# First stage of a fused attention, FFN and experts kernel: one hand-written order of single-engine parts for all engines

## The chip, the cores and the metric

The kernel runs on one core of a Trainium2 chip. The metric is device time in microseconds (us): the median of several runs of the whole program.

## What is computed

A bidirectional attention between tokens and 32 state slots, a two-layer FFN with g = h - tanh(h), and a gated mixture of eight experts, all in float32:

```python
scores = scale * x @ state.T          # softmax over slots, then a @ state
scores2 = scale * state @ x.T         # softmax over tokens, then a2 @ x
x = concatenate([xread, sread])       # 2304 tokens, 512 wide
h = x @ w_in                          # 512 -> 2048
x = (h - tanh(h)) @ w_out             # 2048 -> 512
out = sum over e of P[:, e] * (relu(x @ w1[e]) @ w2[e])
```

There are B = 4 batches of H = 8 heads, S = 512 tokens, D = 64.

## The kernel before, in words

Products run with float32r operands that are split into a high and a low part, so each is three matmuls (`mm3`, lines 92 to 95: high by high, low by high, high by low). The FFN is cut into NJ = 8 slices j of 256 columns. Slice j = 0 is run together with the attention; that is the first stage, and the one that the change touches.

**Attention of a batch** (class `Attention`, lines 265 to 363). `tokens(p)` turns two heads of x on TensorE (tile xtps) and copies them out (xt). `scores(q)` multiplies them with the state (sc2ps), copies the result (sc) and takes the largest (mx). `over_slots(half)` turns the scores (sc1ps), takes the largest over slots (m) and subtracts it (e). `exps` does the exponentials on ScalarE, the sums and reciprocals on VectorE and the share e times m on GpSimd (L320). `back(q)` turns the other softmax (e2ps, e2t). `weights(q)` turns the shares (atps) and splits them: ath on ScalarE (L89), then atl = atps - ath on VectorE (L90). `read(q)` multiplies the token softmax with x (srps) and writes four narrow pieces of 32x64 into yacc_s, scaled by sm, on ScalarE (L359).

**First products.** `emit_m(j, bp, q)` multiplies w_in with the state of a pair of batches (mps; mh on ScalarE, ml on VectorE). `emit_h(j, b, i)` multiplies ath, atl with mh, ml (hps) and makes the gate t = h - tanh(h) and its split gh, gl. `emit_y(0, b, d)` multiplies gh, gl with w_out (yps) and copies the sum to yacc. `emit_xs` and `emit_hs` do the same for the 128 state rows (xsps, hsps), and `emit_ts` turns their gate (tsps). The first tsps of the program comes at the end of the stage.

**Weight pieces.** The weights of the FFN come as 64-bit words in pieces of 128x256. `prep()` (lines 155 to 206) is one step of a pipeline over pieces: ScalarE makes mag and low (L203, L204), VectorE makes mag, low and bits (L187, L194, L190), GpSimd adds (L198), ScalarE casts the high part (L182), GpSimd subtracts for the low part (L165). Each slice takes 8 pieces; `prep_done` and `tick` call prep ahead of their use.

**What sets the order.** The steps of the stage are written batch by batch (`first_unit`, lines 580 to 617): while a batch's attention is finished the next one is begun. Each step holds work of several engines. The program is put in order by a planner with a timeline of its own, which moves instructions within what their data allow; `anchor` and `behind` keep some prep steps behind the last instruction traced on ScalarE and VectorE. x of batches 0 and 1 is loaded on SP (`load_x`, L224), and the state on ScalarE's DMA queue (L232); the state rows are copied into slb by four VectorE and four ScalarE copies (L241). The first ScalarE copy also brings an ACT_TABLE_LOAD.

After the first stage, slices 1 to 7 of the FFN and then the experts follow; those loops are not touched, except for the bound that `most` sets for prep, which is written in other units.

## Time and profile before

| | us |
|---|---|
| median of 3 runs | 1790.05 (1788.44 to 1791.13) |
| the profiled execution | 1788.31 |
| its span | 1786.5 |
| TensorE busy in the span | 1753.3 (98%) |
| VectorE busy | 1188.8 (67%) |
| ScalarE busy | 803.5 (45%) |
| GpSimd busy | 1191.6 (67%) |

The span is the stretch that the profile sees on the core; the execution's own time is 1.8 us more. PE is TensorE, PEld its weight loads, DVE VectorE, ACT ScalarE, POOL GpSimd, SP the queue that issues most DMAs. The busy shares are over the whole span; the first stage is its first 118.7 us, in which the engines stand otherwise.

### The profile page before, as it was taken

What the parts mean: (1) busy time and instruction counts of PE and PEld (TensorE: products, weight loads), DVE (VectorE), ACT (ScalarE), POOL (GpSimd) and SP (SyncE); (2) the same over time, 40 slices, a digit from 0 to 9 for tenths busy, and PEclk for the clock granted to TensorE, in tenths of its full rate; (3) what the DMA queues carried; (4) which work ended last, traced back from release to release, by engine and by line L of the source; (5) the groups of instructions that cost most, each with busy time, mean ns of one, the idle gap of its engine ahead of it and who ended that gap; (6) DMA issues with size and microseconds to landing.
All of it is one profiled execution on the core that took longest, in us unless ns stands there. A gap on an engine that the chain in (4) does not pass through costs nothing.

```text
span 1786.5 us, 23142 instructions
## 1 busy us (share of the span) xinstructions
PE 1753.3 (98%) x8181; PEld 1444.3 (81%) x8181; DVE 1188.8 (67%) x1762; ACT 803.5 (45%) x1429; POOL 1191.6 (67%) x1041
## 2 busy tenths in 40 slices
PE   7899999999999999999999999999999999999998
PEld 4578888877888888888888888888888888888887
DVE  6688887555876666666666666856666666666665
ACT  7877666545233323333232333344444445444442
POOL 3366555457777767666667776557777777777774
PEclk9999999999999999999999999999999999999999
DMA  5311110007666666555665665555555655645541
GB/s 142 90 59 66 59 48 19 0 30 238 208 204 218 212 206 204 197 196 202 203 199 192 203 212 188 195 200 200 218 184 189 234 181 190 230 175 202 212 183 53
DMA packets 158695, 296.73 MB, mean 166 GB/s; under 512 B 28340, under 2 KB 107764, under 8 KB 154228
## 3 DMA queue, kind: packets, MB, share of 16 engines
q1 hardware_dynamic: 157540, 295.00, 48.3%
q8 instruction: 64, 1.05, 0.2%
q14 instruction: 51, 0.42, 0.1%
q10 hardware_dynamic: 1040, 0.26, 0.1%
HBM read 174.87 MB, written 120.36 MB: 165 GB/s over the span
## 4 chain that ended last, share of the span: by engine, by line
PE 87%; DVE 6%; ACT 3%; POOL 2%; issue 1%; DMA 1%; DVEq 0%; ACTq 0%
PE p1b L978 14%; PE p_P L1129 14%; PE p1a L978 9%; PE p1c L978 9%; PE p L95 7%; PE p L93 7%; PE p L94 7%; PE yps L94 2%; PE yps L93 2%; PE yps L95 2%; PE p1s L1030 2%; PE mP L1129 2%; DVE low L194 1%; PE hps L95 1%; PE hps L93 1%
## 5 line engine op out<-in xcount | busy, mean ns | idle before, releaser
L771 POOL TENSOR_TENSOR w1l<-w1r,w1h 128x768 fp32r<-128x768 f32 (+1 forms) x96 | 170.9, 1807 | 159.9 <-ACT w1h L769 159.9
L1081 DVE SCALAR_TENSOR_TENSOR oacc<-p,pr,oacc 128x512 f32<-128x512 f32 x224 | 166.2, 744 | 111.9 <-PE p L95 111.9
L978 PE MATMUL p1b<-xT,w1h 128*128 128x512 f32 x768 | 237.6, 390 | 0.0
L1138 DVE TENSOR_TENSOR m<-p_P,m 128x512 f32<-128x512 f32 x232 | 159.3, 688 | 86.8 <-PE p_P L1129 86.8
L93 PE MATMUL p<-w2b,hh 128*128 128x512 f32 x512 | 199.9, 390 | 1.8 <-ACT hh L916 1.5
L94 PE MATMUL p<-w2b,hh 128*128 128x512 f32 x512 | 199.4, 389 | 0.0
L95 PE MATMUL p<-w2b,hl 128*128 128x512 f32 x512 | 197.1, 390 | 0.6 <-DVE hl L917 0.6
L986 DVE TENSOR_TENSOR U<-p1b,P 128x512 f32<-128x512 f32 x128 | 88.4, 690 | 150.2 <-PE p1b L978 128.3
L978 PEld LDWEIGHTS p1b<-xT,w1h 128*128 128x128 f32 x768 | 142.4, 188 | 28.0
L978 PE MATMUL p1a<-xB,w1h 128*128 128x512 f32 x512 | 161.1, 395 | 0.0
L411 POOL TENSOR_TENSOR gl<-t,gh 128x512 fp32r<-128x512 f32 x64 | 86.4, 1361 | 101.8 <-ACT gh L410 100.6
L978 PE MATMUL p1b<-xT,w1l 128*128 128x512 f32 x384 | 149.6, 390 | 0.0
L806 ACT CAST w2s<-w2r 128x1024 fp32r<-128x1024 f32 x32 | 33.7, 1052 | 229.6 <-POOL w2r L800 229.6
L935 POOL TENSOR_TENSOR h11l<-U,h11h 128x512 fp32r<-128x512 f32 x32 | 41.4, 1294 | 126.8 <-ACT h11h L934 82.1
L917 DVE SCALAR_TENSOR_TENSOR hl<-U,hh 128x512 fp32r<-128x512 f32 x64 | 101.2, 1581 | 27.9 <-ACT hh L916 27.9
L1136 ACT COPY m<-p_P 128x512 f32<-128x512 f32 x128 | 74.9, 586 | 99.9 <-PE p_P L1129 99.6
L93 PEld LDWEIGHTS p<-w2b,hh 128*128 128x128 f32 x512 | 96.1, 188 | 23.0 <-ACT hh L916 2.6
L95 PEld LDWEIGHTS p<-w2b,hl 128*128 128x128 f32 x512 | 96.1, 188 | 21.1 <-DVE hl L917 1.3
L768 POOL TENSOR_TENSOR w1r<-w1r 128x256 f32<-128x256 f32 x128 | 94.2, 746 | 27.1 <-DMA w1r<-in_moe_w_dram 24.2
L94 PEld LDWEIGHTS p<-w2b,hh 128*128 128x128 f32 x512 | 96.1, 188 | 19.7
L986 DVE TENSOR_TENSOR U<-p1c,U 128x512 f32<-128x512 f32 x128 | 87.7, 685 | 33.6 <-PE p1c L978 33.3
L978 PEld LDWEIGHTS p1a<-xB,w1h 128*128 128x128 f32 x512 | 93.7, 188 | 17.8
(297 smaller groups left out, 4810.2 us busy)
## 6 DMA issues: line engine op xcount, KB each, us to landing
w1h<-w1h SPq DMA_DIRECT2D x64, 896.0 KB, 4.3
w1l<-w1l SPq DMA_DIRECT2D x64, 896.0 KB, 6.1
w<-w2a SPq DMA_DIRECT2D x30, 1024.0 KB, 4.8
w<-w2c SPq DMA_DIRECT2D x30, 768.0 KB, 7.6
w1r<-in_moe_w_dram SPq DMA_DIRECT2D x128, 128.0 KB, 4.4
w2r<-in_moe_w_dram SPq DMA_DIRECT2D x32, 512.0 KB, 4.0
w2a<-w2b SPq DMA_DIRECT2D x60, 256.0 KB, 3.3
w2c<-w2s SPq DMA_DIRECT2D x60, 256.0 KB, 3.9
```

Of the source, the lines that this page charges most:

```text
L93: nc.tensor.matmul(ps, whi, xhi, start=start, stop=False, **k)
L94: nc.tensor.matmul(ps, whi, xlo, start=False, stop=False, **k)
L95: nc.tensor.matmul(ps, wlo, xhi, start=False, stop=stop, **k)
L411: nc.gpsimd.tensor_tensor(out=lo, in0=g, in1=f32(hi), op=ALU.subtract)
L768: nc.gpsimd.tensor_tensor(out=r[:, out], in0=r[:, a], in1=r[:, b], op=op)
L771: nc.gpsimd.tensor_tensor(out=lo[:, c0:c1], in0=r[:, c0:c1], in1=f32(hi[:, c0:c1]), op=ALU.subtract)
L917: nc.vector.scalar_tensor_tensor(out=lo, in0=src, scalar=0.0, in1=f32(hi), op0=ALU.max, op1=ALU.subtract)
L978: nc.tensor.matmul(t[z], w[:, slot, k, :], x[:, m, k, :], start=(first and k == i == 0), stop=(k == 1 and i == 2), skip_group_check=True,)
L986: nc.vector.tensor_tensor(out=t[name], in0=a, in1=b, op=ALU.add)
L1081: nc.vector.scalar_tensor_tensor(out=o, in0=ps, scalar=w, in1=o, op0=ALU.mult, op1=ALU.add)
L1129: nc.tensor.matmul(ps, w[:, a], b, start=(i == 0 and not goes_on), stop=(i == 2 and (last or not kept)), skip_group_check=True,)
L1138: nc.vector.tensor_tensor(out=m, in0=ps, in1=m, op=ALU.add)
```

## The change

All steps of the first stage are cut into parts that each hold work of one engine (`words_of`, `bits_of`, `number_of`, `hi_of`, `lo_of` for a weight piece; `tokens` and `keep_tokens`, `weights`, `weights_hi` and `weights_lo`, and so on for the attention and the products). A table of 440 words, ORDER_OF_FIRST, names them in one order: a word is the part's letter, the batch (or slice and batch) and an index, and at times the engine that does it (A, V or G). `listed` runs a part with each of its instructions pinned behind the last instruction traced so far on its engine, for all five engines, so that the parts of the table keep their order on every engine. Other instructions may still be moved between them by the planner.

The work itself is the same but for these: of the copies out of PSUM, 4 of 16 of xt, 3 of 8 of e2t (1 of 8 before) and 4 of 16 of yacc are done by DVE; 20 of the 32 narrow products into yacc_s move from ACT to DVE; one of the eight state copies moves to DVE; a copy of one column of `ones` at the start brings the ACT table load ahead of the state copies; x of batches 0 and 1 is loaded by head, 8 DMAs each, batch 1 first (before: 8 halves for batch 0, 4 DMAs for batch 1). The pieces 0 to 15 are in the table; prep goes on from piece 16. Batches 1 and 0 are run interleaved, then 2 and 3.

```diff
         live = {}
-        at = [0]
-        rest = [-1] * 4
-        steps_of = [*range(KD), *rest, *range(KD, 2 * KD), *rest, *range(2 * KD, len(pieces))]
+        FIRST_PIECES = 4 * KD
+        at = [FIRST_PIECES]

         def piece(step):
-            return steps_of[step] if 0 <= step < len(steps_of) else -1
+            return step if FIRST_PIECES <= step < len(pieces) else -1

...
+        def words_of(n):
+            v = live[n]
+            nc.scalar.activation(temp(n, "mag", F32, 2), f32(v["raw"][:, :, 1]), AF.Abs, scale=REBASE)
+            nc.scalar.mul(temp(n, "low", U32, 3), v["raw"][:, :, 0], 2.0 ** -29)
...
+        def number_of(n):
+            v = live[n]
+            nc.gpsimd.tensor_tensor(out=v["bits"], in0=v["bits"], in1=v["low"], op=ALU.add)
...
-                )
-                nc.gpsimd.tensor_tensor(out=t, in0=t, in1=v["low"], op=ALU.add)
-            n = piece(step)
-            if n >= 0:
-                fetch(n + AHEAD)
-                v = live[n]
-                nc.scalar.activation(temp(n, "mag", F32, 2), f32(v["raw"][:, :, 1]), AF.Abs, scale=REBASE)
-                nc.scalar.mul(temp(n, "low", U32, 3), v["raw"][:, :, 0], 2.0 ** -29)
+            for part, behind in (((lo_of,), 4), ((hi_of,), 3), ((bits_of, number_of), 1), ((words_of,), 0)):
...
         def prep_done(n):

-            while at[0] < n + 12:
+            while at[0] < n + 4:
                 prep()


...
+        def load_x(b, i):
+
             if b not in x_t:
                 x_t[b] = att.tile([P, NT, H, D], F32, tag="x", bufs=2, name=f"x{b}")
-            for h in range(0, H, heads):
-                for t in range(NT):
-                    nc.sync.dma_start(
-                        x_t[b][:, t, h:h + heads], x[b, h:h + heads].rearrange("h (p t) d -> t p h d", t=NT)[t]
-                    )
-                yield
+            if b > 1:
+                nc.sync.dma_start(x_t[b][:, i], x[b].rearrange("h (p t) d -> t p h d", t=NT)[i])
+            else:
+                nc.sync.dma_start(x_t[b][:, :, i], x[b, i].rearrange("(p t) d -> p t d", t=NT))
...
         for be in range(2):
             for r in range(4):
                 u, w = divmod(r, 2)
                 to = 2 * ((u + be) % 2) + w
-                (nc.scalar.copy if be else nc.vector.tensor_copy)(
+                (nc.scalar.copy if be and r else nc.vector.tensor_copy)(
                     slb[NS * to:NS * (to + 1), :, u::2, w * D:(w + 1) * D], srow[NS * r:NS * (r + 1), be::2]
                 )
-        for n in range(AHEAD + 3):
-            fetch(n)
-        run(load_x(1), 9)
-
...
             def weights(self, q):
-                b = self.b
-                ps = bank(f"atps{b}_{q}")
+                ps = self.ps["w", q] = bank(f"atps{self.b}_{q}")
                 for t in range(NT):
                     g = self.e1[t // 2][0].rearrange("a g s -> a (g s)")
                     o = (t % 2) * 256 + q * P
                     nc.tensor.transpose(ps[:, t * P:(t + 1) * P], g[:, o:o + P], ident)
-                hi = ffn.tile([P, S], F32R, tag="ath", bufs=B * NQ, name=f"ath{b}_{q}")
-                lo = ffn.tile([P, S], F32R, tag="atl", bufs=B * NQ, name=f"atl{b}_{q}")
-                split_ps(ps, hi, lo)
-                at_t[b, q] = hi, lo
+
+            def weights_hi(self, q):
+                hi = ffn.tile([P, S], F32R, tag="ath", bufs=B * NQ, name=f"ath{self.b}_{q}")
+                lo = ffn.tile([P, S], F32R, tag="atl", bufs=B * NQ, name=f"atl{self.b}_{q}")
+                at_t[self.b, q] = hi, lo
+                nc.scalar.copy(hi, self.ps["w", q])
+
+            def weights_lo(self, q):
+                hi, lo = at_t[self.b, q]
+                nc.vector.tensor_tensor(out=lo, in0=self.ps.pop(("w", q)), in1=f32(hi), op=ALU.subtract)

...
+            def keep_read(self, q, by_scalar):
+                b, ps = self.b, self.ps.pop(("r", q))
                 for r in range(4):
                     h = 4 * q + 2 * ((r // 2 + b) % 2) + r % 2
-                    nc.scalar.mul(
-                        sr[NS * b:NS * (b + 1), h * D:(h + 1) * D],
-                        ps[NS * r:NS * (r + 1), r % 2 * D:(r % 2 + 1) * D],
-                        self.sm[NS * r:NS * (r + 1), q:q + 1],
-                    )
-
...
+        def y_first(b, d):
+            ps = laid[0, b, d] = acc_bank(f"yps0_{b}_{d}")
+            for i in range(2):
+                wh, wl = wo_t[i]
+                mm3(ps, wh[:, d * P:(d + 1) * P], wl[:, d * P:(d + 1) * P], *g_t[0, b, i], i == 0, i == 1)
+
+        def y_keep(b, d, copy):
+            copy(yacc[b][:, d, :], laid.pop((0, b, d)))

...
-        def first_unit(b):
...
-        def anchor():
-            for z, e in (("ACT", mybir.EngineType.Activation), ("DVE", mybir.EngineType.DVE)):
-                last[z] = next(i for i in reversed(nc.cur_bb.bb.instructions) if i.engine == e)
-
-        def behind(fn):
-
-            with tc.issue_after(last["ACT"]), tc.issue_after(last["DVE"]):
+        att_t = {}
+        ENGINES = [getattr(mybir.EngineType, z) for z in ("PE", "Activation", "DVE", "Pool", "SP")]
+
+        def listed(fn):
+
+
+            traced = nc.cur_bb.bb.instructions
+            with ExitStack() as pins:
+                for e in ENGINES:
+                    mine = next((i for i in reversed(traced) if i.engine == e), None)
+                    if mine is not None:
+                        pins.enter_context(tc.issue_after(mine))
                 fn()

-        for b in range(-1, B - 2):
-            for n, step in enumerate(first_unit(b)):
-                step()
-                if n == 5 if b < 0 and at[0] < 16 else n % 4 == 3:
-                    anchor()
-                if b < 0 and at[0] < 16 and n > 5:
-                    behind(prep)
-                elif (b >= 0 or n > 5) and n % 4 == 3:
-                    behind(tick)
-        for step in first_unit(B - 2):
-            step()
-        for j in range(NJ):
...
+            PARTS[z] = lambda b, n, fn=fn: fn(10 * b + n)
+        PARTS["Y"] = y_first
+        PARTS["x"] = load_x
+
+        ORDER_OF_FIRST = """
+            x16 x10 x12 x11 x14 x13 x17 x15 F02 T10 U00 t10A F01 U10 u00 v00 x01 T11 v10 u10 T13 x03 t11A V10
+            x02 t13A T12 V00 S10 A02 x00 t12V x05 A01 I02 S11 x06 c10 I01 F03 j02 c11 T01 F12 C02 m10 j01 O10
...
+            q40 Y32 y30A Y33 y32A y33A
+        """
+        for word in ORDER_OF_FIRST.split():
+            listed(lambda: PARTS[word[0] + word[3:]](int(word[1]), int(word[2])))
+        att_ctx.close()
+        emit_ts(0)
+        emit_hs(1)
+        for j in range(1, NJ):
             more = j + 1 < NJ
-            if j:
-                most[0] = 8 * (j + 2) + 2 + 11
+            most[0] = 8 * (j + 2) + 2 + 3
             if not more:
                 mid_ctx.close()
                 x2p = ctx.enter_context(right("x2p", reuse_waits="tile"))
...
@@ -669,24 +778,12 @@
                     [lambda: emit_logits_of_operands(1)], [lambda: emit_logits(2)],
                 ]
             for b in range(B):
-                if j == 0 and b < B - 1:
-                    continue
                 steps = {d: [] for d in range(KD)}
                 if b + 1 < B:
                     steps[0] += [lambda i=i: emit_h(j, b + 1, i) for i in range(2)]
                 elif more:
-                    steps[0 if j else 2] += [lambda i=i: emit_h(j + 1, 0, i) for i in range(2)]
-                if j == 0:
-                    emit_xs()
-                    att_ctx.close()
-                    emit_hs(0)
-                    most[0] = 29
-                    prep_done(16)
-                    for q in range(NQ):
-                        steps[0].append(lambda q=q: emit_m(1, 0, q))
-                        steps[1].append(lambda q=q: emit_m(1, 1, q))
-                    steps[3].append(lambda: emit_ts(0))
-                elif more and b == B - 2:
+                    steps[0] += [lambda i=i: emit_h(j + 1, 0, i) for i in range(2)]
+                if more and b == B - 2:
                     prep_done(8 * (j + 1) + KD)
                     for q in range(NQ):
                         steps[q].append(lambda q=q: emit_m(j + 1, 0, q))
```

Three places show how instructions move. In the rows a name ends in its index and a number of its buffer.

DVE, batch 1's attention weights (atl is the low part of the weights, ath the high part that ACT casts just before; m and e are the softmax over slots, mx the largest score, ml the low part of the first product; mag, low and bits belong to a weight piece). Before:

```order
L318 TENSOR_SCALAR m_1_1_512<-m_1_1_512 128x16
L190 TENSOR_SCALAR bits_595<-mag_537 128x256
L319 RECIPROCAL m_1_0_503<-m_1_0_503 128x16
L319 RECIPROCAL m_1_1_512<-m_1_1_512 128x16
L90 TENSOR_TENSOR atl_0_619<-atps_0_613,ath_0_618 128x512
L90 TENSOR_TENSOR atl_1_635<-atps_1_629,ath_1_634 128x512
L187 TENSOR_SCALAR mag_602<-mag_602 128x256
```

Now:

```order
L306 TENSOR_REDUCE mx_0_203<-sc2ps_1_330 128x1
L161 TENSOR_SCALAR mag_320<-mag_320 128x256
L164 SCALAR_TENSOR_TENSOR low_322<-raw_256,low_322 128x256
L168 TENSOR_SCALAR bits_371<-mag_320 128x256
L322 TENSOR_REDUCE m_0_1_385<-sc1ps_1_359 128x16
L310 TENSOR_SCALAR mx_0_203<-mx_0_203 128x1
L391 TENSOR_TENSOR atl_0_388<-atps_0_375,ath_0_387 128x512
L328 TENSOR_TENSOR e_0_1_411<-sc1ps_1_359,m_0_1_385 128x512
L391 TENSOR_TENSOR atl_1_403<-atps_1_380,ath_1_402 128x512
L450 TENSOR_TENSOR ml_1_392<-mps_1_1_393,mh_1_391 64x512 x2
```

Before, the two atl follow the reciprocals of their own batch; now parts of batch 0 (mx_0, m_0, e_0) and a weight piece stand between them.

PE, the end of the stage (yps is the second product of the FFN, hps the first one of the next slice, tsps the turn of the state rows' gate, hsps the state rows' product of slice 1). Before:

```order
L94 MATMUL yps_3_3_1363<-gl_3_1_1160,woh_441 128x512
L95 MATMUL yps_3_3_1363<-gh_3_1_1159,wol_442 128x512
L93 MATMUL hps_0_0_1320<-ath_1_331,mh_0_1241 128x512
L94 MATMUL hps_0_0_1320<-atl_1_332,mh_0_1241 128x512
L93 MATMUL hps_0_1_1334<-ath_0_322,mh_0_1241 128x512
```

Now:

```order
L95 MATMUL hps_0_0_1245<-ath_1_630,ml_0_1046 128x512
L93 MATMUL yps_1_0_1255<-gh_1_0_692,woh_664 128x512
L94 MATMUL yps_1_0_1255<-gl_1_0_693,woh_664 128x512
L95 MATMUL yps_1_0_1255<-gh_1_0_692,wol_665 128x512
L93 MATMUL yps_1_0_1255<-gh_1_1_593,woh_640 128x512
L94 MATMUL yps_1_0_1255<-gl_1_1_594,woh_640 128x512
L95 MATMUL yps_1_0_1255<-gh_1_1_593,wol_641 128x512
L559 MATMUL tsps_1308<-ident,ts_1091 128x128 x2
```

Before, only batch 3's second product was left at the end of the stage; now products of batch 1 (yps_1) come as late as that, and some of batch 3 come behind tsps.

DVE, behind the last atl of the stage, where no attention is left (t is the gate; the pieces with raw_1383 and up are numbers 16 and up, which belong to slice 2). Before:

```order
L90 TENSOR_TENSOR atl_1_1098<-atps_1_1092,ath_1_1097 128x512
L518 MEMSET wg 128x512
L523 MEMSET wg_both 128x512
L530 TENSOR_TENSOR add<-ident 16x8
L90 TENSOR_TENSOR xs_lo<-xsps,xs_hi 128x512
```

Now, some rows further on:

```order
L164 SCALAR_TENSOR_TENSOR low_1389<-raw_1383,low_1389 128x256
L468 TENSOR_TENSOR t_3_1_1136<-hps_3_1_1103,t_3_1_1136 128x512
L161 TENSOR_SCALAR mag_1387<-mag_1387 128x256
L168 TENSOR_SCALAR bits_1415<-mag_1387 128x256
L450 TENSOR_TENSOR ml_1_1144<-mps_1_0_1145,mh_1_1143 64x512 x2
L516 COPY yacc_80<-yps_2_3_1167 128x512
L161 TENSOR_SCALAR mag_1424<-mag_1424 128x256
```

The planner puts pieces 16 and up, which are not in the table, between the table's parts here, and the xs and wg instructions now stand ahead of the last atl. From the middle of slice 1 on, the instructions stand alike in both programs on every engine.

## Rows read from the trace of the kernel before

**Rows 1.** The page's first part: busy time, share and instructions of each engine.

```profile
PE 1753.3 (98%) x8181; PEld 1444.3 (81%) x8181; DVE 1188.8 (67%) x1762; ACT 803.5 (45%) x1429; POOL 1191.6 (67%) x1041
```

**Rows 2.** Windows: stretch, its length, busy of PE, PEld, DVE, ACT, POOL, clock, DMA.

```profile
0.00:14.60 14.60, 7.39 (x29) 4.57 (x30) 6.20 (x14) 7.14 (x14) 1.56 (x8) 1.00 1.03 228
14.60:102.40 87.80, 72.28 (x433) 51.50 (x431) 61.16 (x143) 71.42 (x173) 38.12 (x44) 0.92 0.34 89
102.40:118.60 16.20, 15.90 (x88) 13.58 (x89) 14.07 (x26) 14.39 (x34) 8.43 (x10) 1.00 0.10 30
118.60:162.00 43.40, 42.97 (x214) 36.25 (x213) 38.07 (x67) 31.38 (x72) 28.01 (x30) 1.00 0.19 63
```

**Rows 3.** The chain that ended last, 98 to 120 us: start, us, what.

```profile
101.11 0.59 ACT ath L89
101.73 0.70 DVE atl L90
...
116.01 0.23 PE yps L95
...
118.73 0.23 PE tsps L452 x2
```

**Rows 4.** Waits, 14.6 to 102.4 us: total, times, longest.

```profile
DVE atl L90 <- ACT ath L89: 16.9, 3, 7.5
...
DVE mx L290 <- ACT sc L288: 5.8, 4, 2.3
...
DVE m L303 <- PE sc1ps L299: 2.8, 1, 2.8
```

**Rows 5.** Timeline of DVE, 48 to 64 us: start, us, instruction, [idle before, releaser].

```profile
52.95 0.36 DVE L319 RECIPROCAL m<-m 128x16 f32<-128x16 f32 x2
60.78 1.29 DVE L90 TENSOR_TENSOR atl<-atps,ath 128x512 fp32r<-128x512 f32 x2 [7.47 <-ACT ath L89]
```

**Rows 6.** DVE's groups, 0 to 118.6 us: count, busy, mean ns, idle before.

```profile
L194 DVE SCALAR_TENSOR_TENSOR low<-raw,low 128x256 uint32<-128x256 uint32 x22 | 11.4, 525 | 0.1
...
L187 DVE TENSOR_SCALAR mag<-mag 128x256 f32<-128x256 f32 x23 | 10.1, 447 | 0.5 <-ACT mag L203 0.4
L190 DVE TENSOR_SCALAR bits<-mag 128x256 uint32<-128x256 uint32 x22 | 9.9, 461 | 0.5 <-POOL wil L165 0.3
...
L291 DVE TENSOR_SCALAR mx<-mx 128x1 f32<-128x1 f32 x8 | 1.2, 151 | 0.2
...
L331 DVE COPY e2t<-e2ps 128x512 f32<-128x512 f32 x1 | 0.7, 676 | 0.0
...
L518 DVE MEMSET wg<- 128x512 f32 x1 | 0.5, 485 | 0.1
```

**Rows 7.** ACT's groups, 0 to 118.6 us.

```profile
L203 ACT ACTIVATE mag<-raw 128x256 f32<-128x256 f32 x24 | 10.3, 439 | 0.1
...
L359 ACT ACTIVATE yacc_s<-srps,sm 32x64 f32<-32x64 f32 x32 | 9.8, 305 | 5.4 <-PE srps L353 3.3 <-issue 1.7
...
L279 ACT COPY xt<-xtps 128x512 f32<-128x512 f32 x16 | 9.2, 596 | 2.2 <-PE xtps L277 2.2
L436 ACT COPY yacc<-yps 128x512 f32<-128x512 f32 x16 | 8.5, 592 | 3.8 <-PE yps L95 3.7
...
...
L241 ACT ACT_TABLE_LOAD x1 | 1.3, 1283 | 5.0 <-DMA yacc<-in_state_dram 5.0
```

**Rows 8.** Timeline of SP's queue, 0 to 30 us.

```profile
0.74 5.03 SPq L224 DMA_DIRECT2D x<-in_x_dram  x8
...
8.26 5.21 SPq L224 DMA_DIRECT2D x<-in_x_dram  x4
```

**Rows 9.** Tile bits, 0 to 118.6 us: duration ns min/median/max, first and last start.

```profile
L190 DVE TENSOR_SCALAR bits<-mag x22: 278/285/1385, 12.9 to 116.8; 128x256 uint32<-128x256 uint32 x22
```

**Rows 10.** Windows of the two stretches at the lower clock.

```profile
25.60:32.40 6.80, 6.24 (x23) 5.41 (x24) 6.61 (x13) 5.02 (x14) 2.06 (x3) 0.50 0.16 49
...
52.90:59.80 6.90, 4.91 (x30) 3.94 (x32) 0.40 (x3) 2.85 (x7) 2.73 (x3) 0.51 0.12 40
```

More of the change, by code (lines that the diff above doesn't have):

```diff
@@ L199, in prep @@
-            n = piece(step)
-            if n >= 0:
-                fetch(n + AHEAD)
-                v = live[n]
-                nc.scalar.activation(temp(n, "mag", F32, 2), f32(v["raw"][:, :, 1]), AF.Abs, scale=REBASE)
-                nc.scalar.mul(temp(n, "low", U32, 3), v["raw"][:, :, 0], 2.0 ** -29)
+            for part, behind in (((lo_of,), 4), ((hi_of,), 3), ((bits_of, number_of), 1), ((words_of,), 0)):
+                n = piece(step - behind)
+                if n >= 0:
+                    if not behind:
+                        fetch(n)
+                        fetch(n + AHEAD)
+                    for fn in part:
+                        fn(n)
@@ L234, in attention_ffn_experts @@
         )
-        for _ in first:
-            pass
+        nc.scalar.copy(ones[:, :1], ones[:, :1])
         for be in range(2):
@@ L305, in over_slots @@
[L305 to L322 removed]
+                self.ps["o", half] = v, m
@@ L571, in turn_logits @@
             )
-        most = [3 * KD + 2 + 12]
+        most = [0]
         def tick():
@@ new lines, in of_batch, with part @@
+        def of_batch(name, *more):
+            def part(b, n):
+                if b not in att_t:
+                    att_t[b] = Attention(b)
+                getattr(att_t[b], name)(n, *more)
+            return part
+        COPY = {"A": nc.scalar.copy, "V": nc.vector.tensor_copy}
+        ON = {"V": nc.vector, "G": nc.gpsimd}
+        PARTS = {z: of_batch(name) for z, name in (
[3 rows of a table added]
+        )}
+        for z, copy in COPY.items():
+            PARTS["t" + z] = of_batch("keep_tokens", copy)
+            PARTS["b" + z] = of_batch("keep_back", copy)
+            PARTS["g" + z] = of_batch("keep_read", z == "A")
+            PARTS["y" + z] = lambda b, d, copy=copy: y_keep(b, d, copy)
```

329 lines of the change are left out of this document (183 added, 146 removed), and 3 rows, old and new, of the table PARTS.

## The prediction

> **What bounds the kernel now.** I read the page first: PE is busy in 98% of the span [rows 1], so the stages behind the first give nothing back and pass a gain on whole; they keep their instructions. Then the windows by stage, which show that the first stage is another matter. I cut it at three points. Until 14.6 us the data arrive and the first scores are made. From there to 102.4 lies the attention: it ends with the last atl, which runs from 101.73 for 0.70 [rows 3]. From 102.4 to 118.6 only products are left, and at 118.73 the first tsps starts [rows 3], which I take as the end of the stage in both programs. In the middle stretch of 87.80 us ACT is busy for 71.42 (81%), PE for 72.28, DVE for 61.16 (70%) [rows 2]: no engine is full. The waits say why. DVE idles 87.80 - 61.16 = 26.6 us, of which 16.9 stand in three waits of atl for ath, 5.8 in four of mx for the score copy, 2.8 in one of m [rows 4], together 25.5. The longest is seen in DVE's timeline: it ends batch 1's reciprocals at 53.3 and does nothing for 7.47 us, until ath is there at 60.78 [rows 5]. Softmax, turn, cast and split follow one another in one batch, and the queue holds nothing else that could run. So the stage is bound by chains that hand over from engine to engine.
>
> **The change, term by term.** I sum against the profiled execution, 1788.31 us; it is 1.74 below the median of 1790.05, which I add again at the end. PE's matmuls are the same in number and kind, so are POOL's instructions; what changes is the place.
>
> *DVE in the attention part.* Counted in the two orders up to the last atl, DVE loses 9 low, 8 mag and 6 bits, since only 12 pieces are done there (before some 20): 9 x 0.525 + 8 x 0.447 + 6 x 0.461 = 11.1 us [rows 6]. It gains 7 wide copies, 7 x 0.676 = 4.7 (e2t's copy, rows 6), and 20 narrow products. DVE's price for these is not in the trace: below lies mx of one column with 0.151 [rows 6], above ACT's price for the same piece, 0.305 [rows 7], so 3.0 to 6.1. I take 0.22, between them, because DVE's wide operations cost about what ACT's do: 4.4. One more state copy, the two fills of wg (0.485 each, rows 6) and xs_lo, which now stand earlier, make 2.0. So 11.1 go and 11.1 come, and DVE keeps its 6.20 + 61.16 = 67.4 us [rows 2].
>
> *ACT and PE there.* ACT loses 15 mag and low at 0.44, 16 narrow products at 0.305, 4 xt copies at 0.596 and 9 yacc copies at 0.592 [rows 7], 19.2 us, and some 4 us of smaller moves: of its 78.6 us [rows 2] about 56 stay. Of the 96 matmuls of the second product, PE does 24 there instead of 72: 48 at 0.23 [rows 3], 11.0 us less. So DVE becomes the busiest engine and sets the length.
>
> *How much DVE still idles.* This term decides. In the new order parts of the other batch and a weight piece stand between reciprocals and atl; the two batches of a pair alternate, so the wait of one is filled by the other. Bounds: 0, if every wait is filled; 26.6, if all stay. The nearest rows are those where DVE has independent work: in 102.4 to 118.6 it idles 2.1 of 16.2 us, in 118.6 to 162 5.3 of 43.4, 12 to 13% [rows 2], and there PE holds it up. I take a quarter of 26.6, 6.6 us, which is a tenth of the new stretch.
>
> *Lead-in.* ACT_TABLE_LOAD stands between the landing of the state and ACT's state copies with 1.28 us [rows 7]; it moves ahead of the landing. The x loads limit what follows: 8 issues took 5.03 us, the 4 larger ones of batch 1 5.21 [rows 8], so 16 small ones cost SP the same, and the first batch arrives no sooner. I count 1.0 of the 1.28: 14.6 becomes 13.6. The weight pieces are issued later now, behind batch 1's x; their first use (mps) is behind both batches' scores, which hides that. If that cover fails, the first mps waits for the issues that are now ahead of its pieces, 0.63 us for each (5.03 / 8).
>
> *End of the attention part:* 13.6 + (67.4 - 6.2) + 6.6 = 81.4, where before 102.4 stood: -21.0.
>
> *The products behind it.* They took 16.2 us, PE busy for 15.90 [rows 2]. The 11.0 us of deferred second products come on top: 27.2. DVE does 14.07 now, and gets some 10 us of pieces 16 and up, which the planner hoisted; less gates and fills it has about 22 in 27.2 and stays covered. If a hoisted piece stands ahead of a gate that PE needs, that cover is gone; I add 0.5. Then tsps starts at 81.4 + 27.2 + 0.5 = 109.1, against 118.7: **-9.6 us**. Slice 1 gets the same pieces as before, so nothing is given back there. 1788.31 - 9.6 = 1778.7 for the profiled execution, with the 1.74 **1780.4 us** for the median.
>
> *The clock.* In two stretches of 6.8 and 6.9 us the granted clock was 0.50 and 0.51 [rows 10], the level of 1.2 GHz; PE was busy 6.24 and 4.91 us in them. At the full clock half of that, 5.6 us, would be saved if it lay on the path. In the new attention part DVE sets the length, so I count 0 and keep 5.6 for a rival. The Trainium skill (TensorE: Matmul & The Clock Gate, What's actually happening) has the low clock as the default that activity releases; by it a denser PE would lose both falls, and the sum would be nearer to that rival.
>
> **Rivals.**
>
> *B, the fill is nearly complete and DVE gets cheaper.* bits took 0.461 us in the mean, but 0.285 in the median and up to 1.385 [rows 9]: some of the piece operations are stretched. In the attention part their number falls to 36, and POOL has a third fewer pieces to do there. If all 36 were stretched as bits is and none of it were left, 36 x 0.176 = 6.3 us would go; with the idle time at 3 instead of 6.6 and the clock kept up the gain is 9.6 + 3.6 + up to 6.3, 13 to 19.5: 1770.5 to 1777, say 1774. Against it: the stage gets shorter and POOL's 48.1 us [rows 2] do not, so both are busy together more of the time.
>
> *C, the busiest engine alone counts.* Before, ACT with 78.6 us made an attention part of 102.4; DVE with 67.4 at the same share makes 87.8, and with 27.7 behind it 115.5: -3.2, 1786.9, within what can be told from no change. The Trainium skill (Perfetto Trace Analysis, Identifying the Most-Contended Engine) has kernels improve by their most-contended engine, and by that rule this would be the result. For it: balancing moved 11 us on to DVE. Against it: the longest waits stand on an engine that was not the busiest.
>
> *D, slower: the fixed order brings its own waits.* A part that is late holds everything behind it on its engine, and the planner may no longer go around it. The place is DVE behind ACT's casts: narrow products wait for PE's reads, atl for ath, with the other batch's largest scores behind them. If as much idle time is left as before (26.6), the attention part ends at 13.6 + 61.2 + 26.6 = 101.4, and 27.7 behind it makes 129.1: +10.4, 1800. It decides from 16.2 us of idle time on, where the sum is zero.
>
> *E, the hoisted pieces hold up the gates.* Half of their 10 us on PE's path in the last stretch makes 109.1 + 5 = 114.1: -4.6, 1785.4.
>
> That the order is not followed is excluded: the orders of the engines show it.
>
> **How the numbers follow.** My forecast A (idle time from 4 to 10 us) has 0.50, B 0.22, C 0.12, E 0.08, D 0.08. A measurement of this kernel can tell about 0.2%, 3.6 us, from no change, so faster begins below 1786.5. A, B and E lie there: 0.80; C makes 0.12 for the same, D 0.08 for slower. The range of A is 1777 to 1784. The range goes down to 1771, into B but not to its end, and up to 1788, over E and C; D and the ends of B and C are left out, some 0.18.
>
> **What would show it.** Right: the first tsps near 109 us and the last atl near 81; DVE's idle time between 13.6 and there under 10, no wait of atl over 2 us; the stage's gain equal to the gain of the span within 1 us. Wrong: a last atl behind 90 with waits of DVE for ACT in the list (C or D), an early last atl with a tsps that does not follow within 29 us (E), or a later stage that idles longer than before.

## The result, and the profile after

The changed kernel takes **1775.39 us** (median of 6 runs, 1774.96 to 1775.92), the kernel before, on the same chip, 1790.49 (6 runs, 1787.95 to 1791.13): ratio 0.9919, 95% interval 0.9906 to 0.9932, so 15.1 us less. Of the profiled executions, before took 1788.31 with a span of 1786.5 and the changed one 1775.18 with 1773.4: 13.1 us less.

The first part of the page of the changed kernel, beside [rows 1]:

```profile
span 1773.4 us, 23139 instructions
PE 1747.0 (99%) x8181; PEld 1441.1 (81%) x8181; DVE 1201.2 (68%) x1793; ACT 794.3 (45%) x1399; POOL 1193.5 (67%) x1041
```

As many matmuls, but PE is busy for 6.3 us less. PE's busy time counts the matmuls at the low clock with their longer duration, and one of the two falls of [rows 10] is gone (below). Half of the busy time in the falls is what they add: 5.6 us before, 1.7 now, so 3.9 of the 6.3; the rest is not accounted for.

To say where the 13.1 us come from, a mark is needed at which both programs have done the same work. The first turn of the token sums (tsps), which the prediction took, is not such a mark. In the order of PE's matmuls, 24 second products (yps) that stood ahead of it before stand behind it now; at the second turn 7 matmuls still do (1 yps, 6 of the state rows' ysps); at the third the two programs have run the same matmuls. PE's timeline around the three turns, before and after:

```profile
118.57 0.38 PE L452 MATMUL tsps<-ident,ts 128*128 128x128 f32 x2
125.53 0.38 PE L452 MATMUL tsps<-ident,ts 128*128 128x128 f32 x2
166.92 0.38 PE L452 MATMUL tsps<-ident,ts 128*128 128x128 f32 x2
```

```profile
99.16 0.38 PE L559 MATMUL tsps<-ident,ts 128*128 128x128 f32 x2
111.07 0.38 PE L559 MATMUL tsps<-ident,ts 128*128 128x128 f32 x2
154.03 0.38 PE L559 MATMUL tsps<-ident,ts 128*128 128x128 f32 x2
```

Third turn: 166.92 - 154.03 = **12.9 us**, beside 13.1 of the span. So the whole gain lies ahead of it, and the later slices keep it. At the first turn, with 24 x 0.227 = 5.4 us added for the missing products, it is 118.57 - (99.16 + 5.4) = 14.0: 1.1 us are given back between the first turn and the third.

The windows of the changed kernel, cut at 13.6 (the prediction's lead-in), at the end of the last atl, and at the three turns (stretch, length, busy time of PE, PEld, DVE, ACT, POOL, clock, DMA), beside [rows 2]:

```profile
0.00:13.60 13.60, 7.69 (x36) 5.57 (x37) 7.00 (x17) 7.65 (x16) 1.51 (x8) 1.00 0.86 206
13.60:79.10 65.50, 57.93 (x408) 42.61 (x405) 63.58 (x150) 55.08 (x126) 30.35 (x35) 0.97 0.34 95
79.10:99.20 20.10, 18.06 (x86) 14.22 (x85) 19.35 (x42) 17.74 (x44) 13.80 (x18) 1.00 0.35 119
99.20:111.10 11.90, 10.38 (x53) 8.48 (x52) 11.87 (x20) 7.95 (x20) 8.71 (x9) 1.00 0.27 90
111.10:154.00 42.90, 42.90 (x208) 36.16 (x207) 35.27 (x60) 30.23 (x68) 26.48 (x30) 1.00 0.15 50
```

Read DVE's column. Where it idled 26.6 of 87.8 us, it now idles 65.50 - 63.58 = **1.9 of 65.5**, 0.8 of the next 20.1 and nothing up to 111. No other engine is full before 111. From there on PE is.

The waits say the same. All waits of DVE that the view lists between 13.6 and 79.1 (total, times, longest), beside [rows 4]:

```profile
DVE atl L391 <- ACT ath L387: 0.5, 1, 0.5
DVE xt L292 <- PE xtps L288: 0.2, 1, 0.2
```

Of 25.5 us in eight waits 0.7 in two are left. PE's waits from 79.1 to the third turn are now these:

```profile
PE hps L93 <- DVE gsl L90: 1.5, 1, 1.5
PE hps L95 <- DVE ml L450: 1.1, 1, 1.1
PE yps L94 <- POOL gl L494: 1.0, 1, 1.0
```

DVE's groups from 0 to 80 us, beside [rows 6] (count, busy, mean ns, idle before):

```profile
L164 DVE SCALAR_TENSOR_TENSOR low<-raw,low 128x256 uint32<-128x256 uint32 x13 | 6.5, 501 | 0.0
L413 DVE TENSOR_SCALAR yacc_s<-srps,sm 32x64 f32<-32x64 f32 x20 | 5.6, 281 | 0.3
L168 DVE TENSOR_SCALAR bits<-mag 128x256 uint32<-128x256 uint32 x13 | 5.6, 431 | 0.0
...
L161 DVE TENSOR_SCALAR mag<-mag 128x256 f32<-128x256 f32 x14 | 5.2, 370 | 0.0
```

A narrow product takes 0.281 us on DVE; on ACT it took 0.305 [rows 7]. The window runs a little past the last atl: ahead of that, 12 low, 12 mag and 12 bits are done, where the kernel before does 21, 20 and 18 ahead of its last atl.

The clock: one of the two falls of [rows 10] is gone, one of 3.4 us (34.5 to 37.9) is left, again behind a stretch in which PE idled for more than half. (In the kernel before PE was busy for 1.49 of the 3.60 us ahead of the first fall, and for 1.13 of the 2.90 ahead of the second.) Two windows of the changed kernel:

```profile
31.00:34.40 3.40, 1.45 (x19) 1.15 (x20) 3.28 (x6) 3.33 (x8) 0.00 (x0) 1.00 0.06 14
34.40:37.60 3.20, 3.20 (x19) 2.69 (x16) 3.12 (x10) 1.86 (x5) 0.73 (x1) 0.51 0.00 0
```

Last, the place of the batches. DVE's timeline of the kernel before, of the last batch's largest scores (mx) and of the last two atl:

```profile
85.94 0.69 DVE L290 TENSOR_REDUCE mx<-sc2ps 128x1 f32<-128x512 f32 x1 [0.79 <-ACT sc L288]
...
101.73 1.29 DVE L90 TENSOR_TENSOR atl<-atps,ath 128x512 fp32r<-128x512 f32 x2 [4.79 <-ACT ath L89]
```

The same of the changed kernel:

```profile
59.11 1.28 DVE L306 TENSOR_REDUCE mx<-sc2ps 128x1 f32<-128x512 f32 x2
...
78.41 0.67 DVE L391 TENSOR_TENSOR atl<-atps,ath 128x512 fp32r<-128x512 f32 x1
```

Before, the last atl starts 16.4 us after the last batch's last mx (two run from 101.73 on, the second from about 102.3); now 18.7 after it (the second mx starts at 59.71). One batch did not get shorter. Its scores are taken 26 us earlier.

### The profile page after: what moved, and what is told of

It is laid out like the page before. It is cut to its first block, busy times and chain, and to the rows that moved or that the text cites. A ratio compares the mean times of both kernels' runs of the same rounds, so it can differ in the third digit from the quotient of the medians.

```text
span 1773.4 us, 23139 instructions
## 1 busy us (share of the span) xinstructions
PE 1747.0 (99%) x8181; PEld 1441.1 (81%) x8181; DVE 1201.2 (68%) x1793; ACT 794.3 (45%) x1399; POOL 1193.5 (67%) x1041
## 4 chain that ended last, share of the span: by engine, by line
PE 86%; DVE 7%; ACT 3%; POOL 2%; issue 1%; DMA 1%; SPq 0%; DVEq 0%; ACTq 0%; POOLq 0%
PE p1b L1075 14%; PE p_P L1226 14%; PE p1a L1075 10%; PE p1c L1075 9%; PE p L95 7%; PE p L93 7%; PE p L94 7%; PE p1s L1127 2%; PE yps L94 2%; PE yps L93 2%; PE mP L1226 2%; PE yps L95 2%; DVE low L164 2%; PE hps L95 1%; DVE bits L168 1%
## 5 line engine op out<-in xcount | busy, mean ns | idle before, releaser
L1083 DVE TENSOR_TENSOR U<-p1c,U 128x512 f32<-128x512 f32 x128 | 87.9, 686 | 33.3 <-PE p1c L1075 33.0
```

The lines of the kernel that those rows point to most:

```text
L1083: nc.vector.tensor_tensor(out=t[name], in0=a, in1=b, op=ALU.add)
```

## The experiments

**Theory:** the stage was bound by hand-overs within one batch. The gain comes from the order, which puts the other batch's parts between them, until DVE's sum is the bound. **Rivals:** the new shares of DVE and ACT made it (balance); splitting the parts made it and the pins did nothing; or it is only that the weight pieces moved behind the attention.

All runs at a glance: the median, its ratio to the kernel before on the same chip with its 95% interval, the end of the last atl and the start of the third turn in the profiled execution. In every run the span minus the third turn is 1619.0 to 1620.2 us, so what a run gains or loses in its profiled execution lies ahead of the third turn. The runs come from several chips, on which the kernel before took 1788.34 to 1790.92 us, so a difference of 1 to 2 us between two lines is to be read from the ratios.

| run | us | ratio | last atl | third turn |
|---|---|---|---|---|
| before | 1790.49 | | 103.0 | 166.92 |
| changed | 1775.39 | 0.9919 [0.9906, 0.9932] | 79.1 | 154.03 |
| 20 narrow products on DVE, order of before | 1790.86 | 1.0009 [1.0000, 1.0018] | 104.7 | 169.00 |
| no pins | 1783.17 | 0.9961 [0.9946, 0.9976] | 90.9 | 161.96 |
| no pins, pieces held | 1784.52 | 0.9971 [0.9961, 0.9982] | 92.6 | 163.63 |
| only DVE pinned | 1781.29 | 0.9952 [0.9937, 0.9967] | 85.4 | 160.32 |
| 16 parts back on ACT | 1781.30 | 0.9946 [0.9930, 0.9963] | 82.4 | 159.68 |
| 5.4 us more on DVE | 1779.99 | 0.9942 [0.9927, 0.9957] | 83.3 | 158.17 |
| 4.7 us more on ACT | 1776.37 | 0.9923 [0.9908, 0.9938] | 81.0 | 155.86 |
| table load late | 1776.41 | 0.9926 [0.9914, 0.9938] | 80.6 | 155.53 |
| less on DVE | 1778.55 | 0.9939 [0.9927, 0.9952] | 79.5 | 157.04 |
| gate's weights pinned | 1776.23 | 0.9927 [0.9915, 0.9939] | 78.1 | 154.21 |
| gate's weights and first turn pinned | 1775.63 | 0.9920 [0.9907, 0.9934] | 78.3 | 154.50 |
| gate's weights pinned, pieces held | 1774.37 | 0.9920 [0.9906, 0.9934] | 78.5 | 153.60 |

### Narrow products on DVE, on the kernel before

```diff
-                    nc.scalar.mul(
+                    (nc.scalar.mul if (b, q) in ((0, 0), (1, 1), (3, 0)) else nc.vector.tensor_scalar_mul)(
```

> The kernel before, with 20 of its 32 narrow products put on DVE instead of ACT (6 us off the busiest engine), nothing else. Theory (the kernel before waits on chains and not on ACT's sum): within 2 us of the kernel before, either way. Rival (balance alone): 4 to 8 us faster than the kernel before.

Ratio 1.0009: nothing gained. ACT's 71.4 us in the attention part became 65.2, and the idle time changed its name. DVE's waits from 14.6 to 104.7 us of this run:

```profile
DVE yacc_s L359 <- PE srps L353: 12.0, 3, 5.3
DVE mx L290 <- ACT sc L288: 5.7, 4, 2.3
DVE m L303 <- PE sc1ps L299: 2.4, 1, 2.4
```

Before, 16.9 us stood at atl [rows 4]; now DVE waits within the batch at another station, at the narrow product for srps. So taking 6 us off ACT gains nothing in the old order. The wide copies that the change also moves from ACT to DVE were not moved here; that the rival falls for them too is argued, not shown.

### No pins

```diff
-            listed(lambda: PARTS[word[0] + word[3:]](int(word[1]), int(word[2])))
+            PARTS[word[0] + word[3:]](int(word[1]), int(word[2]))
```

> The same parts, emitted in the same order, on the same engines, but the planner may reorder them (the pins are gone). Theory (the gain is DVE's queue being kept full by the fixed order): waits of DVE come back, DVE idles over 8 us between 13.6 and the last atl instead of 1.9, the time goes back to between 1780 and 1790 us. Rival (splitting into single-engine parts and the new shares of the engines are enough): within 2 us of 1775.4.

1783.17: 7.8 us lost against the changed kernel, 7.7 kept against the kernel before (1790.92 on this run's chip). So the pins are worth about half. The other half belongs to the cut into parts, with the table as the order of writing, together with the new shares, loads and bound for prep, which this run keeps; no run takes these apart. DVE's idle time is not what came back most. The attention part of this run:

```profile
13.60:90.90 77.30, 60.05 (x410) 44.20 (x409) 71.09 (x172) 61.20 (x144) 37.62 (x45) 0.96 0.37 108
```

It idles 6.2 us (the theory asked for over 8). The stretch is longer mainly because DVE works 7.5 us more in it: the planner put more weight pieces there. Ahead of the last atl 21 low are done instead of 12, and as the table has only 16 pieces, at least five of them are of numbers 16 and up. That left two readings, that these pieces cost the time or that the order does, and the next run was made for them.

### No pins, and the pieces held behind the last atl

```diff
+        held = []
...
         def prep():
+            with ExitStack() as pins:
+                for i in held if at[0] < 40 else []:
+                    pins.enter_context(tc.issue_after(i))
+                prep_step()
...
+            if word == "l30":
+                for e in ENGINES[1:3]:
+                    held.append(next(i for i in reversed(nc.cur_bb.bb.instructions) if i.engine == e))
```

> As the run without pins, but the weight pieces 16 and up may be issued only behind the last atl, as in the changed kernel; within the first stage the planner still orders freely. In the run without pins 8 such pieces (21 low instead of 13, about 8.5 us of DVE) had moved ahead of the last atl, at 90.9. Theory (those pieces are what the free order pays for, not the order among the attention's own parts): last atl at 82 to 84, 1775 to 1779 us. Rival (the hand-made order inside the stage is what counts): 1781 us or more.

The theory was wrong: 1784.52, and the last atl ends at 92.6, later still. With the pieces from 16 on gone (16 low are left), DVE idles 79.10 - 67.03 = 12.1 us:

```profile
13.60:92.70 79.10, 62.55 (x410) 44.80 (x410) 67.03 (x162) 59.90 (x140) 35.73 (x43) 0.94 0.33 92
```

The reason is in DVE's timeline of this run:

```profile
75.06 0.69 DVE L314 TENSOR_REDUCE mx<-sc2ps 128x1 f32<-128x512 f32 x1 [4.37 <-PE sc2ps L307]
76.52 0.69 DVE L314 TENSOR_REDUCE mx<-sc2ps 128x1 f32<-128x512 f32 x1 [0.59 <-ACT sc L311]
...
91.96 0.68 DVE L399 TENSOR_TENSOR atl<-atps,ath 128x512 fp32r<-128x512 f32 x1
```

The planner takes the last batch's scores at 75 to 77, the fixed order at 59 to 61. From there a batch needs 15.4 us here (91.96 - 76.52), 16.4 in the kernel before, 15.3 without pins (74.87 to 90.20). So the pieces were filling, not the cause: in these runs the end of the attention is late where the scores of the last batch stand late, whatever fills DVE meanwhile.

### Only DVE's order pinned

```diff
-        ENGINES = [getattr(mybir.EngineType, z) for z in ("PE", "Activation", "DVE", "Pool", "SP")]
+        ENGINES = [getattr(mybir.EngineType, z) for z in ("DVE",)]
```

> The changed kernel with only DVE's order pinned; the planner orders PE, ACT, POOL and the loads freely around it. Theory (the order of DVE's queue is the one that counts, as it is the bound): 1775 to 1778 us. Rival (PE's and ACT's order have to fit it, as every atl needs its ath and every largest score its scores): 1780 us or more, with waits of DVE for PE or ACT.

1781.29, on the rival's side. DVE now waits 6.8 us from 13.6 to 85.5, of which 3.2 for the turned x on PE. Behind the last atl PE waits for ml, and the clock falls (PE's timeline, then two windows):

```profile
100.97 0.77 PE L93 MATMUL hps<-ath,mh 128*128 128x512 f32 x1 [3.93 <-DVE ml L450]
```

```profile
95.00:100.00 5.00, 2.04 (x12) 1.60 (x10) 4.79 (x9) 4.93 (x12) 3.80 (x6) 0.98 0.38 120
100.00:105.00 5.00, 3.52 (x8) 2.38 (x9) 4.88 (x10) 3.46 (x8) 1.60 (x3) 0.50 0.10 39
```

Here an order for the bound engine alone is not enough; the engines that feed it have to follow it.

### Sixteen parts back on ACT

```diff
-t12V ... b10V ... g10V ... y01V ...
+t12A ... b10A ... g10A ... y01A ...
```

> Order and pins as changed, but all 16 parts that were given to DVE (5 of the narrow products, 4 copies of x, 3 wide copies behind the second turn, 4 copies of the second products) go back to ACT; it takes some 10 us off DVE in the attention part and puts 11 on ACT (55 becomes 66). Theory (DVE's total work is the bound now, ACT's 55 us are far below): ACT becomes as long as DVE was, so no gain from it: between 1775 and 1780 us. Rival (the balance made the gain): 1784 us or more, as ACT is the busiest engine again.

1781.30, 5.9 us lost, between the two expectations. With pins, the shares do count: ACT is busy for 63.8 of the 68.8 us up to the last atl (82.4), and DVE waits 15.0 us for it (4.7 at t, 3.2 at mx, 2.8 at mag, 2.6 at atl, 1.7 at m). That is 3.3 us at the last atl. By estimate at most another 1.7 us go behind it, where the clock was 0.95 over 34.1 us (34.1 x 0.05) and PE was not busy throughout. So the new shares are needed in the new order, while the part of them that was tried in the old order gained nothing.

### More work on DVE, and on ACT

```diff
                 nc.vector.reduce_max(self.mx[:, q:q + 1], self.ps["s", q], axis=AX.X)
+                nc.vector.reduce_max(self.mxd[:, q:q + 1], self.ps["s", q], axis=AX.X)
```

> The largest score (0.68 us on DVE) is taken a second time into a column nobody reads, 8 times in the attention part: 5.4 us more on DVE. Theory (DVE is full from 10 to 111 us and sets the length): all of it comes on the end, 4.5 to 6 us, 1780 to 1781.4. Rival (the stage is still bound by the chains between engines or by PE): less than 2 us, below 1777.4.

```diff
                 nc.scalar.copy(self.sc[q], self.ps["s", q])
+                nc.scalar.copy(yacc[self.b][:, KD - 1, :], self.ps["s", q])
```

> The copy of the scores (0.58 us on ACT) is done a second time, into a place that is overwritten later, 8 times in the attention part: 4.7 us more on ACT. Theory (ACT has 10 us to spare in the attention part): less than 2 us, below 1777.4. Rival (every engine's chain counts, as the copy stands between scores and largest slots): 3 to 5 us, 1778.4 to 1780.4.

8 x 0.676 = 5.4 us more on DVE cost 4.6 (1779.99), 4.7 us more on ACT 1.0 (1776.37). DVE is the bound of the new order, ACT is not. Up to the last atl, DVE was busy for 4.0 us more in the first run (74.53 against 70.58), and the last atl moved by 4.2: what is put on DVE is paid in full. All four executions of that run lie above all six of the changed kernel.

In the second run the last atl moved by 1.9, but not all of this is ACT's work. Its four executions fall into two pairs: 1775.40 and 1775.65 us at a mean granted clock of 1.000, and 1777.09 and 1777.82 at 0.998. The first pair lies within the changed kernel's 1774.96 to 1775.92. The profiled execution is one of the second: its clock was 0.50 from 33.1 to 39.8 us, for twice as long as in the changed kernel. So the work added on ACT costs 1.0 us at most, and by the first pair next to nothing.

### The table load late

```diff
-        nc.scalar.copy(ones[:, :1], ones[:, :1])
```

> The changed kernel without its early copy of a single column, so that the loading of ACT's table falls behind the landing of the state again (1.28 us). The prediction's term for this was 1.0 us. Theory: DVE's first copies start as before and the state copies on ACT end 1.3 us later, the whole stage moves by 0.7 to 1.3 us: 1776.1 to 1776.7. Rival (DVE, which is the bound and does not use the table, hides it): under 0.4 us.

1776.41, 1.0 us more, the size of the term, but the intervals of the two ratios overlap, and the trace speaks against the mechanism. ACT's state copies end 1.35 us later (6.43 against 5.08). The turn of the state on PE (sbps) needs them, but it comes behind the first turns of x in both kernels, at 7.03 and 6.69, and these wait for the landing of x (6.15 and 5.81). So the first mx comes 0.33 later (14.37 against 14.04), as much as x landed later in this execution. The load itself is hidden behind x.

The last atl ends 1.56 later all the same. The clock was 0.50 from 33.3 to 40.1 us here, 6.8 us instead of 3.4. The 16 matmuls of one srps took 1.97 us in it, 1.24 in the changed kernel; ACT then waits 2.09 us for the turned x instead of 1.34; and at the end of the fall DVE waits twice (DVE's timeline):

```profile
39.53 0.69 DVE L344 TENSOR_REDUCE m<-e 128x16 f32<-128x512 f32 x1 [0.84 <-ACT e L340]
41.70 0.69 DVE L291 COPY xt<-xtps 128x512 f32<-128x512 f32 x1 [0.78 <-PE xtps L287]
```

In the changed kernel the first of these waits is not there and the second is 0.24: 1.4 us more, which with the 0.33 covers the 1.56. No run changed the fall alone, but the one execution of this run at a mean clock of 1.000 took 1775.58, within the changed kernel's range.

### A try at a better version: less on DVE

The run with more work suggested that less work on DVE is paid back. Two fills and a sum of the gate's weights went to POOL. One product of the shares (N30) went to POOL too, and eight narrow products (g20, g21) went to ACT:

```diff
-... g20V ... g21V ... N30V ...
+... g20A ... g21A ... N30G ...
```

> The changed kernel with less on DVE ahead of the first token sum: the two fills of the gate's weights and the sum of two corners of the identity go to POOL (1.4 us), one product of the shares too (1.07), and two of DVE's five narrow reads to ACT (8 products, 2.25 us): 4.7 us off DVE, 3.2 on POOL, 2.4 on ACT. Theory (DVE's work sets the stage, the run with 5.4 us more cost 4.6): 3 to 4.5 us gained, 1771 to 1772.4. Rival (POOL's additional work stretches DVE's operations, or the chain through POOL is late for the last atl): less than 1.5 us gained or a loss.

1778.55, **3.2 us slower** instead of 3 to 4.5 faster. The edit takes 4.7 us off DVE by the trace of the changed kernel. Up to the last atl only 3.4 of them are gone (67.18 against 70.58): the same 36 operations on weight pieces took 17.5 us instead of 16.1, a stretching such as the rival expected; that POOL's added work made it is not shown. And the last atl ends at 79.5, no earlier, as DVE idles 5.4 us instead of 1.9. Of this 2.6 us are waits for ath on ACT, which now has the eight narrow products. The loss comes behind it, on PE (PE's timeline, and two windows):

```profile
96.51 0.50 PE L93 MATMUL hps<-ath,mh 128*128 128x512 f32 x1 [0.65 <-ACT mh L446]
99.31 0.50 PE L95 MATMUL hps<-ath,ml 128*128 128x512 f32 x1 [2.07 <-DVE ml L450]
```

```profile
95.00:100.00 5.00, 2.29 (x9) 1.28 (x8) 4.92 (x13) 4.89 (x11) 1.78 (x3) 1.00 0.46 142
100.00:105.00 5.00, 5.00 (x21) 4.08 (x20) 4.97 (x10) 2.66 (x7) 4.44 (x4) 0.66 0.42 128
```

PE idles 2.7 of 5 us, then the clock is 0.66 over 5 us in which PE is busy throughout: by estimate 5 x 0.34 = 1.7 us lost on the path. The order of ml and the pieces on DVE there is the planner's.

### Three more tries at it

The gate's weights pinned where they are written, late, which takes 1.58 us off DVE and gives nothing to another engine:

```diff
-                load_gate()
+                listed(load_gate)
```

> The changed kernel with the preparation of the expert gate's weights (two fills, a sum, a split: 1.58 us of DVE, which the planner had put between 75.8 and 79.8) pinned to the place in which it is written, before the last slice. No other engine gets work. Theory (DVE sets the stage up to 111 us): the last atl 1.3 to 1.6 us earlier and 0.8 to 1.6 us gained, 1773.8 to 1774.6. Rival (what stands behind the last atl decides, a wait of PE there takes it back or a new fall of the clock as in the run with less on DVE): 1775.4 or more.

1776.23. The last atl ends 1.0 us earlier (78.1), and nothing of it arrives: PE waits 1.69 us for ml at 96.6, and the clock is 0.66 from 95 to 100. The result is on the rival's side. Then, besides:

```diff
-        emit_ts(0)
+        listed(lambda: emit_ts(0))
```

> As the run with the gate's preparation pinned, and the first token sum's turn pinned behind the first stage's last second products, so that its bank isn't held while gsl stands behind weight pieces on DVE (PE waited 1.5 us for gsl at 103.45). Theory: that wait goes, 1 to 1.5 us more gained: 1772.5 to 1773.5. Rival (DVE's sum is the bound there, another of PE's waits for DVE takes its place): no better than the run with the gate's preparation pinned, within 0.5 us.

1775.63: less than the theory asked for. The wait for gsl that it was to remove is not in the trace, but it was already gone in the run before; the one for ml (1.66) and the fall behind it (0.71 from 95 to 100) are nearly as they were. Last, without that, the hold from above, behind the table's last part (ACT's word y33A):

```diff
+                for i in held if 16 <= at[0] < 40 else []:
...
+            if word == "y33A":
```

> The run with the gate's preparation pinned, and besides the weight pieces 16 and up may be issued only behind the last instruction that the fixed order holds on ACT and DVE (near 105 us); some 12 of them had moved ahead of that point, to between 85 and 105, ahead of the second split of the slice's products (ml) and of the first token sum's split (gsl), for which PE waited 1.7 and 1.5 us, in one run with a fall of the clock behind it. They come into slice 1 instead, where DVE has some 7 us to spare in 43. Theory (behind the last atl it is the pieces' place on DVE that costs): the waits for ml and gsl and the fall of the clock go, 1.5 to 3.5 us less than 1775.4: 1772 to 1774. Rival (DVE's sum up to the third token sum is the bound, so the pieces only move the wait into slice 1): 1775 or more.

1774.37 (1774.31 to 1775.38), ratio 0.9920 [0.9906, 0.9934]: with the changed kernel's 0.9919 no difference can be told. The time lies between the two expectations. In the trace the waits for ml and gsl and the fall behind them are gone, and a new wait stands in slice 1 (PE's timeline):

```profile
132.53 0.50 PE L93 MATMUL yps<-gh,woh 128*128 128x512 f32 x1 [1.76 <-DVE yacc L544]
```

Its third turn is at 153.60 instead of 154.03. So the work on DVE up to there has to be done at some time, as the rival said. None of the four versions beats the change by an amount that these runs can tell.

## Why the prediction was right, and where not

The direction and the range held: 1780.4 was forecast (1771 to 1788), 1775.39 measured. The result lies outside forecast A's own range (1777 to 1784), though; it is held by the part of the range that was added for rival B. Step by step:

- **No engine is full, chains bind the stage.** Right. Taking 6 us off ACT gave nothing in the old order, and in the new one the waits fell from 25.5 to 0.7 us. Rival C, with its 1786.9, falls by the result. The Trainium skill (Perfetto Trace Analysis, Identifying the Most-Contended Engine) has kernels improve by the engine with the highest occupancy. In the kernel before, 6 us off that engine gained nothing; in the changed kernel, where DVE is full, 5.4 us more on it cost 4.6. By these runs the rule holds once an engine is full, and not before.
- **The lead-in, 1.0 us.** The run without the early load gave 1.0 too, but this is luck: the load is hidden behind the landing of x, the first mx moved by 0.33 with x, and the rest of that run's loss stands at two waits behind a longer fall of the clock. By this trace the term should have been near 0.
- **DVE's work stays 67.4 us.** 70.6 (7.00 + 63.58). The count of 12 pieces was right. The narrow products took 0.281, inside the bounds but not 0.22 (20 x 0.061 = 1.2 us). Another 0.6 is the cut at 102.4, which lay that much ahead of the end of the last atl (DVE's work up to there was 67.98). The remaining 1.4 is spread over small terms.
- **ACT keeps about 56 us, and PE becomes free.** ACT kept 62.7 (7.65 + 55.08), and PE did 30 second products there, not 24. Neither binds: DVE waited 0.7 us for the two together.
- **DVE idles a quarter of 26.6, 6.6 us.** This is the term that was mis-sized: 1.9. The prediction took the share of later stretches in which PE holds DVE up; here nothing held it up. Together with the larger work, the attention part ended at 79.1 instead of 81.4, 2.3 us better.
- **27.7 us behind it.** At equal work 104.6 - 79.1 = 25.5, 2.2 better. In PE's order 28 matmuls more than counted stand ahead of the last atl: 6 second products, 12 hsps and 4 turns of the state rows, and 6 mps. So PE's work behind it is 18.06 + 5.4 = 23.5 us instead of 15.90 + 11.0 = 26.9, 3.4 less. Against that stand 2.0 us of PE's waits, where the prediction had 0.3 + 0.5.
- **Slice 1 gives nothing back.** 1.1 us came back, with the wait for gsl of 1.5, behind weight pieces on DVE. This is rival E in small.
- **The mark.** Taking the first tsps as the stage's end in both programs was wrong: it moved by 19.4 us and the span by 13.1, so the prediction's sign "equal within 1 us" fails there and holds at the third turn (12.9).
- **The clock at 0.** One of the two falls went, one stayed. The second fall, in the stretch of DVE's 7.47 us of waiting, went where PE became denser, the first stayed in a shorter form. By the Trainium skill (TensorE: Matmul & The Clock Gate, What's actually happening), activity releases the low clock; the trace agrees for one of the two. No run changed the clock alone, but the fall that stayed is not in every trace. In the traces of the runs with less on DVE and with the first turn pinned, PE was busy for the same 1.46 of 3.40 us from 31.0 on, and the clock stayed at 1.00. With the first turn pinned (no fall) the last atl ended at 78.3, without that pin (a fall of 3.4 us) at 78.1: in these two a fall of this length cost nothing, as the prediction counted. The falls of 6.8 us in the runs with more on ACT and with the late table load stand beside a last atl that is 1.6 to 1.9 us later. Behind the last atl a fall is not free either: 1.7 us by estimate in the run with less on DVE.
- **Sum.** 9.6 forecast; 2.3 + 2.2 - 1.1 = 3.4 on top make 13.0, measured 13.1. The rest of the 5.0 us between forecast and result comes of the 1.74 that the prediction added from execution to median: before's runs spread over 3.2 us, and its profiled execution lay low among them; the changed kernel's spread over 1.0, with its own only 0.2 below the median.
- **Rivals.** B named the outcome (1774) and half of the cause, the full filling. Its other half, cheaper pieces, was small: low 501 against 525 ns, mag 370 against 447, bits 431 against 461, for 13 to 14 of each 1.8 us. D did not come; its waits appear in small where the order of one engine does not fit the others, 6.8 us with DVE alone pinned.

## What to carry to other kernels

Where no engine is full, read which hand-overs the idle time stands at, and look when the last independent chain begins: in every run here the last atl starts 15 to 20 us after the last batch's largest scores, and in the changed kernel these are taken at 59.7 instead of 85.9. That this start is the cause is read from the traces side by side; no run moved it alone. Moving work between engines gained something here only once the order had filled one of them. Compare two orders only at a point at which both have done the same work, and expect that a local improvement of a full order moves the wait: of four tried here none gained what can be told. Before a difference of 1 us is put down to an edit, look whether the granted clock of the executions is the same.

## What the runs showed of the hardware that I had not expected

DVE's operation mag on 128x256 takes 0.287 us in the median of the changed kernel's first 112 us and up to 1.387. Two of them stood ahead of gsl and took 2.69 us together, as long as POOL's two gl beside them. DVE's timeline and POOL's at that place:

```profile
98.84 2.69 DVE L161 TENSOR_SCALAR mag<-mag 128x256 f32<-128x256 f32 x2
101.45 0.28 DVE L168 TENSOR_SCALAR bits<-mag 128x256 uint32<-128x256 uint32 x1
```

```profile
98.59 2.79 POOL L494 TENSOR_TENSOR gl<-t,gh 128x512 fp32r<-128x512 f32 x2
```

The Trainium skill (SBUF — State Buffer, Who interferes with whom) says that DVE and GpSimd share one pair of ports. When DVE runs in a two-port mode, which a `tensor_scalar` can enter, whoever issues first holds the pair for its whole instruction, and the other blocks. The two rows agree with that: each mag ends 0.15 us behind a gl (100.23 and 101.53 against 100.08 and 101.38). No run here shows which mode mag ran in, and none took POOL's work away to prove it.

The fall of the clock behind a pause of PE is the other. In five runs (only DVE pinned, less on DVE, 16 parts back on ACT, and the first two with the gate's weights pinned) a wait of PE for ml of 1.7 to 3.9 us came with a granted clock of 0.50 to 0.83 over a stretch of 5 us there. The length of the wait alone does not decide it: the changed kernel's waits of 1.0 to 1.5 us passed without a fall, and so did the wait of 1.76 us for yacc in the run with the pieces held, with 1.00 from 132.5 to 137.5. Where a fall comes, a wait on PE's path can cost more than its own length, by the estimate above 1.7 us more.
